# First sequence's q and k in 256-byte rows, and a written order for every early job, in a fused attention and feed-forward kernel

## The chip, the cores and the metric

The kernel runs on one core of one Trainium2 chip. The metric is device time in microseconds (us), from the first to the last instruction of the program with what lies around it. All data are 32-bit floats, except the two weight matrices, which arrive as 64-bit floats and are converted on the core.

## What is computed

Two blocks follow each other. The first is attention with a threshold: of each row of scores only those within `tau` of the row's maximum are kept.

```python
batch, n_heads, seq, head_dim = (8, 8, 576, 64)
scores = scale * np.matmul(q, k.transpose(0, 1, 3, 2))
thresh = np.max(scores, axis=-1, keepdims=True) - tau
scores = np.where(scores >= thresh, scores, -1000000000.0)
scores = scores - np.max(scores, axis=-1, keepdims=True)
attn = np.exp(scores)
attn = attn / (np.sum(attn, axis=-1, keepdims=True) + 1e-09)
out = np.matmul(attn, v)
```

The second is a feed-forward block over the 4608 tokens, with `w_in` of 512 x 2048 and `w_out` of 2048 x 512 (both float64):

```python
h = x @ w_in
g = np.where(h > 0.0, h, 1.0 * (np.exp(np.minimum(h, 0.0)) - 1.0))
return g @ w_out
```

## The kernel before

**Tiling.** Two heads make a pair, so there are 8 sequences x 4 pairs = 32 pairs. The 576 rows of a head are four blocks of 128 and a tail of 64, and the two tails of a pair share one step. A step is one block of 128 query rows of a pair: scores on TensorE (`sc`), maximum on VectorE (`max`), bound on GpSimd (`th`), exponential on ScalarE (`exp`), mask with the sum on VectorE (`mask`), sum and reciprocal, then the scaling of the row (`norm`). The weights so made are turned, either by TensorE (`part`, copied out of PSUM by `put`) or by VectorE in 32x32 squares with a trip through DRAM (`turn`, `send`, `landed`), and are multiplied with v (`val` early, `main` later). The results are copied out of PSUM by `values_out` (L733, L739).

**PSUM.** Three banks, `f0`, `f1`, `f2`, serve the feed-forward work. The other five are one tile, named `sc` (`wide[0]` in the code). In the front the scores of a step use its first four banks, and the fifth, called `t`, is lent out. From pair 4 on a tail step (`tails_and_values`, L708 scores, L713 and L721 values) uses banks 1 and 2 for the values of the pair two before it and banks 3 and 4 for its own scores. The scores of a half pair (`wide_scores`, L661) then use all five.

**Who waits for whom in the tile `sc`.** `on_banks` is the helper that all users of that tile pass through. It notes which of the five banks an instruction touches, adds a wait on the last users of those banks, and tells the framework to draw no others between these instructions. `watch` calls it where the destination may lie in that tile:

```python
def watch(made, ap):
    if ap.tensor.name == wide[0].tensor.name:
        on_banks(made, ap)
```

**The front.** The first sequence (pairs 0 to 3), the first two feed-forward chunks, the conversion of the 32 weight pieces and pairs 4 to 8 form the front. In it `early_tasks` keeps a table of jobs, each with an engine, a cost, a due time and what it needs. A list scheduler at build time picks, engine by engine, the next job, and `PR` holds its costs and due times. A weight piece i is `lw` (load, 512 KB), `shift`, `rest`, `add`, `sign`, `end` (L255, L244 or L249, L261, L266, L285). Where the plan of TensorE shows a gap, the scheduler fills it with transposes of the identity matrix that nobody reads (L465, `sc<-ident`, `f<-ident`). q and k are loaded as 32-element pieces of rows (128 bytes) by four DMAs to a tensor and pair (L303) and turned by VectorE (L329, L340). The feed-forward work of the front is 64 halves (L802, L774, L842). Twelve sums for a later stage (`xo`, L956) and 24 more (`in`, L928) run on GpSimd and VectorE.

**The loop.** From the tail step of pair 9 on a loop over the pairs takes over: tail step, `main` part 1, `main` part 0, `wide_scores` of half 0, 14 quarters of feed-forward products (L1491, L1631), `wide_scores` of half 1, 14 quarters. Everything that is not on TensorE is put on an agenda by its time after the matmuls (`at`), moved by the table `MOVED`, and issued in that order. The first matmuls of the values' two parts stand in this order, from `tail_step`:

```python
for part, cost in ((1, 2.2), (0, 1.8)):
    end = on_pe(cost, lambda: loc["main"](part))
    at(end, loc["outs"][part], f"out{part}")
```

In `MOVED` the copies out of part 1 stand at +0.83 us for odd pairs (`fout1`) and at -0.49 us for even ones (`sout1`); those of part 0 at -1.7 us for even ones (`sout0`).

Of the kernel before, what the change touches and what calls it, by code (L numbers as in the profile page):

```python
# [48 lines left out]
PR = {'wait_pe': 0.262,  # L49
 'wait_dve': 0.227,  # L50
 'wait_act': 0.276,
 'wait_pool': 0.0,
 'wait_sp': 0.0,
 'b0': 6.944,
 'p0': 4.249,
 'p1': 6.0,
 'p2': 24.241,
 'off': {'rest': -3.215,
         'prep': -4.66,
         'load': -4.611,  # L60
         'v': -4.074,
         'lw': -12.848,
         'crest': -2.529,
         'cadd': -2.278,
         'csign': -2.436,
         'cend': 9.54,
         'sc': -9.569,
         'max': -9.55,
         'exp': -2.54,
         'th': -3.219,  # L70
         'mask': -2.387,
         'norm': 1.617,
         'su': 3.77,
         'turn': 8.34,
         'fetch': 1.597,
         'part': 10.404,
         'put': 6.049,
         'val': 14.58,
         'valb': 7.639,
         'valsq': 3.622,  # L80
         'out': 2.393,
         'fexp': 7.269,
         'fmin': 1.493,
         'felu': 7.359,
         'fin': 1.533},
 'c0': 14.999,
 'c1': 3.798,
 'c2': 3.935,
 'in0': 13.65,
 'in1': 1.671,  # L90
 'xo0': 7.918,
 'xo1': 2.12,
 'h0': 62.091,
 'h1': 3.55,
 'ch0': 79.679,
 'ch1': 0.437,
 'rest_pool': [10, 11, 14, 22, 28, 3, 4, 6, 8],
 'in_pool': [[0, 0], [0, 1], [0, 2], [1, 1], [3, 1], [4, 0], [4, 1], [4, 2], [5, 0], [5, 1], [5, 2], [6, 0], [6, 1],
             [6, 2], [7, 0]],
 'act_norm': [[0, 0], [1, 0], [1, 1], [10, 0], [11, 0], [13, 0], [13, 1], [14, 0], [15, 1], [17, 0], [18, 0], [18, 1],  # L100
              [2, 0], [3, 0], [4, 0], [4, 1, 1], [4, 2, 0], [4, 4, 0], [5, 0, 0], [5, 1], [5, 1, 0], [5, 4, 0],
              [6, 0, 1], [6, 1, 1], [6, 2, 0], [6, 4, 0], [7, 2, 0], [7, 2, 1], [7, 3, 0], [7, 4, 0], [8, 1, 1],
              [8, 2, 0], [8, 2, 1], [8, 4, 0], [8, 4, 1]],
 'su_act': [[4, 0], [4, 1], [5, 2], [6, 0], [6, 1], [6, 2], [7, 0], [7, 4], [8, 2], 13, 14, 15, 2, 5, 7],
 'xo_n': 12,
 'jit': {},
 'split': 2,
 'warm': 83.985,
 'warm0': 8.0,
 'gap': 0.829,  # L110
 'keep': 0.583,
 'safe': 0.0,
 'idle': 20,
 'dma0': 1.287,
 'dma1': 306.761,
 'pt': 5.24,
 'ph': 9.482,
 'offb': {'prep': -6.011,
          'load': -12.705,
          'v': -14.084,  # L120
          'tail': -2.596,
          'wsc': 2.174,
          'main': 1.279,
          'outv': 3.527,
          'max': -0.056,
          'exp': -8.454,
          'th': 4.556,
          'mask': 4.757,
          'norm': 0.612,
          'su': 0.738,  # L130
          'turn': 4.815,
          'send': 1.309,
          'fetch': 20.101,
          'part': 13.644},
 'part_b': [[4, 0], [4, 2], [5, 1], [5, 2], [6, 3]],
 'squares': [12]}
# [3 lines left out]
def kernel(  # L140
# [19 lines left out]
    T = 32  # L160
# [25 lines left out]
    mains = {pr: wstage.tile([P, TAIL], FP32, name=f"qe{pr}", bufs=1) for pr in range(2)}  # L186
# [14 lines left out]
    pos, keep, far, ntau, ntau0 = (const.tile([P, 1], FP32, name=x) for x in ("pos", "keep", "far", "ntau", "ntau0"))  # L201

    def read_tau():
        nc.vector.tensor_scalar(pos, tau_sb, 0.0, None, ALU.is_ge)
        nc.vector.tensor_scalar(keep, pos, SCALE, None, ALU.mult)
        nc.vector.tensor_scalar(far, pos, -FAR, FAR, ALU.mult, ALU.add)
        nc.vector.tensor_tensor(ntau, tau_sb, far, ALU.max)
        nc.vector.tensor_scalar(ntau, ntau, -1.0, None, ALU.mult)
        nc.vector.tensor_scalar(ntau0, ntau, 1.0 / SCALE, None, ALU.mult)
# [10 lines left out]
    for t in qds + vds_first + vds:  # L220
        nc.gpsimd.memset(t, 0.0)
# [88 lines left out]
    def load_v(pr):  # L310
        b, j = divmod(pr, NPAIR)
        tiles = raws[pr]
        vm = tiles["vm"] = (wstage if pr < 2 else raw).tile([P, 2, NC, D], FP32, name="vm", bufs=2)
        vd = tiles["vd"] = (vds_first if pr < 2 else vds)[pr % NVD]
        for i in range(2):
            vh = v[b, 2 * j + i]
            nc.sync.dma_start(vm[:, i], vh[:MAIN].rearrange("(c p) d -> p c d", p=P))
            r = slice(i * TAIL, (i + 1) * TAIL)
            nc.sync.dma_start(vd[r, r], vh[MAIN:])

    def prep_q(pr):
        src = raws[pr]["qm"].rearrange("p j d -> p (j d)")
        if pr < 2:
            both = squares.tile([P, NT, NCH, T], FP32, name="x").rearrange("p g c n -> p (g c n)")
            qT, firsts[pr] = both[:, :MAIN], both[:, MAIN:]
        else:
            qT = qkp.tile([P, S], FP32, name="qT")
        n = (P, MAIN)[pr] if pr < 2 else S
        nc.vector.transpose(qT[:, :n], src[:, :n])  # L329
        if pr == 1:  # L330
            nc.vector.transpose(mains[pr], src[:, MAIN:])
        pairs[pr] = [qT, None, qds[pr % NQD]]

    def scale_q(pr):
        qT = pairs[pr][0]
        nc.gpsimd.tensor_scalar(qT, qT, keep, 1.0, ALU.mult, ALU.mult)

    def prep_k(pr):
        kT = pairs[pr][1] = firsts[pr] if pr < 2 else qkp.tile([P, TAIL + S], FP32, name="kT")
# [3 lines left out]
    def copy_q(pr):  # L343
        qT, _, qd = pairs[pr]
        for i in range(2):
            r = slice(i * D, (i + 1) * D)
            o, tail = qd[r, i * TAIL : (i + 1) * TAIL], mains[pr][r] if pr < 2 else qT[r, MAIN:]
            if pr == 1:
                nc.gpsimd.tensor_scalar(o, tail, keep[r], 1.0, ALU.mult, ALU.mult)
            else:  # L350
                nc.gpsimd.tensor_copy(o, tail)


    def copy_k(pr):
        kT = pairs[pr][1]
        nc.gpsimd.tensor_copy(kT[D:, :TAIL], kT[D:, S:])
# [18 lines left out]
    def vectors(pr):  # L375
        st = {x: small.tile([P, 2], FP32, name=x) for x in ("mx", "th", "su", "rs")}
        if not pr:
            st["nb"] = wstage.tile([P, 2], FP32, name="nb", bufs=4)
# [30 lines left out]
    def normalize_act(pr, i, h):  # L409
        st = open_steps[pr, i]  # L410
        wv = st["w"][:, h * S : (h + 1) * S]
        nc.scalar.mul(wv, wv, st["rs"][:, h : h + 1])
# [12 lines left out]
    def bound_of(pr, i, h):  # L425
        st = open_steps[pr, i]
        nc.gpsimd.tensor_scalar(st["th"][:, h : h + 1], st["mx"][:, h : h + 1], -1.0, ntau if pr else ntau0, ALU.mult,
                                ALU.add)

    def exp_of(pr, i, h):  # L430
        st = open_steps[pr, i]
        bias = st["mx"][:, h : h + 1]
        if not pr:
            bias = st["nb"][:, h : h + 1]
            nc.scalar.mul(bias, st["mx"][:, h : h + 1], keep)
        e = e_slot()
        o = st[h][:, :, :HALF]
        on_banks(nc.scalar.activation(e, o, AF.Exp, bias=bias, scale=1.0 if pr else keep), o)
# [25 lines left out]
    def transpose(dst, src):  # L464
        watch(nc.tensor.matmul(dst, src, idents[-1], is_transpose=True, skip_group_check=True), dst)  # L465
# [15 lines left out]
    def turn_parts(pr, i):  # L481
# [3 lines left out]
        def to(gs, cs, src, r=slice(0, P)):  # L485
            watch(nc.scalar.copy(wT[r, gs, cs].rearrange("p g c n -> p c g n"), src.rearrange("p c (g n) -> p c g n", n=T)), src)
# [4 lines left out]
        def chunks(c0, c1):  # L491
# [3 lines left out]
            return lambda: to(slice(g0, g0 + NT), slice(c0, c1), rt[:, : c1 - c0])  # L495
# [4 lines left out]
        def tails():  # L500
# [4 lines left out]
            def copies():  # L505
                to(ga, slice(0, NC), rt[:, :, :TAIL])
                to(gb, slice(NC + 1, NCH), rt[:, :, TAIL:])
# [3 lines left out]
        def common():  # L511
# [5 lines left out]
            def copies():  # L517
                cs = slice(NC, NC + 1)
                to(ga, cs, rt[:TAIL, :1, :TAIL], slice(0, TAIL))
                to(ga, cs, rt[TAIL:, 1:2, :TAIL], slice(TAIL, P))  # L520
                to(gb, cs, rt[:, 1:2, TAIL:])
# [6 lines left out]

    def turn(pr, i):
        for part in turn_parts(pr, i):  # L530
            part()()
# [65 lines left out]
    def values(pr, part, pv=None, block=None):  # L597
# [8 lines left out]
        watch(nc.tensor.matmul(pv[:, :n], vd, wT[:, :, NC], start=True, stop=False, skip_group_check=True), pv[:, :n])  # L606
        for c in range(NC):
            for h in range(2):
                g0, g1 = (2 * h, 2 * h + 10) if part else (0, wT.shape[1])
                o = pv[h * D : (h + 1) * D, g0 * T : g1 * T]  # L610
                watch(nc.tensor.matmul(o, vm[:, h, c], wT[:, g0:g1, h * (NC + 1) + c], start=False, stop=(c == NC - 1),
                                       skip_group_check=True), o)
        return lambda: values_out(pr, part, pv, block)
# [24 lines left out]
    def watch(made, ap):  # L638
        if ap.tensor.name == wide[0].tensor.name:
            on_banks(made, ap)  # L640

# [5 lines left out]
    def wide_scores(pr, half):  # L647

        qT, kT, _ = pairs[pr]
        for s in range(2):  # L650
# [5 lines left out]
        for h, s, c, n in ((0, 0, 0, 448), (1, 1, 0, 320), (1, 1, 320, 256), (0, 0, 448, 128),  # L656
                           (1, 0, 0, 256), (0, 1, 0, 384), (1, 0, 256, 320), (0, 1, 384, 192)):
# [27 lines left out]
    def tails_and_values(pr, before):  # L685
# [38 lines left out]
        return values_main, [lambda part=part: values_out(before, part, pv[:, part]) for part in range(2)]  # L724

    def values_out(pr, part, pv, block=None):
        b, j = divmod(pr, NPAIR)
        q0, n = TAIL * part, (3 if part else 2) * NT * T
        if block is not None:
            watch(nc.scalar.copy(xts[b][:, j, block * P : (block + 1) * P], pv[:, :P]), pv[:, :P])  # L730
            return
        o = pv[:, q0 : q0 + 2 * P]
        watch(nc.scalar.copy(xts[b][:, j, part * 2 * P : (part + 1) * 2 * P], o), o)  # L733
# [1154 lines left out]
```

## Time and profile before

| what | us |
|---|---|
| three timed runs | 1311.40, 1313.16, 1315.54 |
| median | 1313.16 |
| profiled execution, first to last instruction (its span) | 1310.6 |
| TensorE, VectorE, GpSimd, ScalarE busy | 1274.6, 1022.3, 782.7, 567.7 |
| first scores on TensorE | 5.96 |
| scores of step 4, of step 19 | 38.2, 126.3 |
| tail step of pair 9, where the loop starts | 288.62 |
| tail steps of pairs 10 and 11 | 327.27, 361.28 |

The profiled execution has no other time than its span; the median of the runs lies 2.56 us above it. All times below are counted from the span's first instruction. PE is TensorE, DVE VectorE, ACT ScalarE, POOL GpSimd, SP the engine that issues most DMAs; L and a number are a line of the kernel.

### The profile page before, as it was taken

What the parts mean: (1) busy time and instruction counts of PE and PEld (TensorE: products, weight loads), DVE (VectorE), ACT (ScalarE), POOL (GpSimd) and SP (SyncE); (2) the same over time, 40 slices, a digit from 0 to 9 for tenths busy, and PEclk for the clock granted to TensorE, in tenths of its full rate; (3) what the DMA queues carried; (4) which work ended last, traced back from release to release, by engine and by line L of the source; (5) the groups of instructions that cost most, each with busy time, mean ns of one, the idle gap of its engine ahead of it and who ended that gap; (6) DMA issues with size and microseconds to landing.
All of it is one profiled execution on the core that took longest, in us unless ns stands there. A gap on an engine that the chain in (4) does not pass through costs nothing.

```text
span 1310.6 us, 22008 instructions
## 1 busy us (share of the span) xinstructions
PE 1274.6 (97%) x6990; PEld 1002.2 (76%) x6990; DVE 1022.3 (78%) x2190; ACT 567.7 (43%) x1224; POOL 782.7 (60%) x1149
## 2 busy tenths in 40 slices
PE   7999989999999999999999999999999999999998
PEld 6677556447878888787878787878787887888887
DVE  5888768889889988898898979897989882545534
ACT  4778643445353444444443535252526260422320
POOL 3776583627657665767485747584758473624523
PEclk8999999999999999999999999999999999999999
DMA  7636678779898988898889898989889875221211
GB/s 142 168 119 177 169 208 239 219 213 264 228 254 221 258 230 237 222 244 244 245 215 253 243 235 228 261 240 246 234 239 258 220 218 179 93 73 58 96 61 33
DMA packets 334484, 261.66 MB, mean 200 GB/s; under 512 B 209952, under 2 KB 295456, under 8 KB 334368
## 3 DMA queue, kind: packets, MB, share of 16 engines
q1 hardware_dynamic: 332432, 259.78, 72.3%
q8 instruction: 55, 0.90, 0.3%
q10 hardware_dynamic: 1936, 0.48, 0.2%
q14 instruction: 61, 0.50, 0.1%
HBM read 168.76 MB, written 91.42 MB: 199 GB/s over the span
## 4 chain that ended last, share of the span: by engine, by line
PE 80%; DVE 7%; DMA 3%; POOL 3%; SPq 2%; ACT 2%; issue 2%; DVEq 0%; POOLq 0%; ACTq 0%
PE f L1631 29%; PE f L1491 28%; PE sc L721 8%; PE sc L661 8%; PE sc L713 2%; DVE mx L668 1%; DMA there<-x 1%; POOL t L956 1%; SPq L303 1%; PE sc L708 1%; PE sc L399 1%; PE f L802 1%; DMA wst<-in_moe_w_out_dram 1%; DVE w_one L682 1%; DVE x L539 1%
## 5 line engine op out<-in xcount | busy, mean ns | idle before, releaser
L668 DVE TENSOR_REDUCE mx<-sc 128x1 f32<-128x576 f32 x252 | 179.2, 748 | 32.5 <-PE sc L661 27.7
L678 ACT ACTIVATE w_one<-sc,mx 128x576 f32<-128x576 f32 x140 | 101.1, 739 | 137.5 <-DVE mx L668 114.0
L674 POOL TENSOR_SCALAR th<-mx,ntau 128x2 f32<-128x2 f32 (+1 forms) x140 | 41.6, 297 | 178.0 <-DVE mx L668 177.9
L407 POOL TENSOR_SCALAR w_one<-w_one,rs 128x576 f32<-128x576 f32 x137 | 111.9, 825 | 52.2 <-DVE rs L462 51.5
L661 PE MATMUL sc<-kT,qT 64*128 64x256 f32 (+5 forms) x896 | 127.0, 417 | 1.5 <-DVE w_one L682 1.5
L661 PEld LDWEIGHTS sc<-kT,qT 64*128 64x128 f32 x896 | 98.3, 186 | 35.2 <-issue 23.1
L1491 PE MATMUL f<-xt,sw 128*128 128x256 f32 x512 | 124.1, 384 | 0.8 <-ACT xt L733 0.5
L1491 PE MATMUL f<-xt,w_in_sb 128*128 128x256 f32 x512 | 122.2, 381 | 1.6 <-ACT g L1552 1.6
L682 DVE SCALAR_TENSOR_TENSOR w_one<-sc,th,w_one 128x576 f32<-128x576 f32 x140 | 109.7, 810 | 16.4 <-ACT w_one L678 12.1
L539 DVE STREAM_TRANSPOSE x<-w_one 128x512 f32<-128x512 f32 (+1 forms) x140 | 99.8, 743 | 20.7 <-POOL w_one L407 12.3
L1491 PEld LDWEIGHTS f<-xt,sw 128*128 128x128 f32 x512 | 93.7, 190 | 20.9 <-issue 5.0
L1491 PEld LDWEIGHTS f<-xt,w_in_sb 128*128 128x128 f32 x512 | 96.2, 190 | 17.1 <-ACT w L1505 2.5
L1631 PE MATMUL f<-w_out_sb,g 128*128 128x256 f32 x448 | 107.1, 382 | 0.0
L1631 PE MATMUL f<-w_out_sb,s 128*128 128x256 f32 x448 | 107.0, 382 | 0.0
L1631 PE MATMUL f<-t,s 128*128 128x256 f32 x448 | 105.8, 379 | 0.0
L1491 PE MATMUL f<-x,w_in_sb 128*128 128x256 f32 x448 | 105.8, 379 | 0.0
L678 ACT ACTIVATE e<-sc,mx 128x576 f32<-128x576 f32 x112 | 81.8, 743 | 53.2 <-DVE mx L668 51.6
L407 POOL TENSOR_SCALAR e<-e,rs 128x576 f32<-128x576 f32 x104 | 76.8, 742 | 40.4 <-DVE rs L462 39.1
L1578 POOL TENSOR_TENSOR s<-g 128x256 f32<-128x256 f32 x104 | 80.6, 781 | 28.1 <-PE f L1631 20.0
L682 DVE SCALAR_TENSOR_TENSOR e<-sc,th,e 128x576 f32<-128x576 f32 x112 | 87.9, 809 | 11.2 <-ACT e L678 8.8
L1631 PEld LDWEIGHTS f<-w_out_sb,g 128*128 128x128 f32 x448 | 84.1, 190 | 13.8 <-issue 2.9
L1631 PEld LDWEIGHTS f<-w_out_sb,s 128*128 128x128 f32 x448 | 84.2, 190 | 13.5 <-issue 2.5
(241 smaller groups left out, 2761.1 us busy)
## 6 DMA issues: line engine op xcount, KB each, us to landing
there<-x SPq DMA_DIRECT2D x444, 144.0 KB, 3.7
wTb<-there SPq DMA_DIRECT2D x56, 576.0 KB, 6.6
wTa<-there SPq DMA_DIRECT2D x55, 576.0 KB, 5.0
sw<-win_sums SPq DMA_DIRECT2D x62, 384.0 KB, 4.3
t<-wout_sums SPq DMA_DIRECT2D x45, 512.0 KB, 5.7
there<-x SPq DMA_DIRECT2D x112, 80.0 KB, 1.9
wTb<-there SPq DMA_DIRECT2D x56, 160.0 KB, 3.4
qm<-in_q_dram SPq DMA_DIRECT2D x124, 72.0 KB, 4.6
```

The costliest lines, as they stand in the source:

```text
L407: nc.gpsimd.tensor_scalar(wv, wv, st["rs"][:, h : h + 1], 1.0, ALU.mult, ALU.mult)
L539: nc.vector.transpose(x[:, :, c0 : c0 + nc_], src.rearrange("p (c g n) -> p g c n", c=nc_, n=T))
L661: on_banks(nc.tensor.matmul(o, qT[r, i * P : (i + 1) * P], kT[r, k0 : k0 + n], start=True, stop=True, skip_group_check=True), o)
L668: on_banks(nc.vector.tensor_reduce(st["mx"][:, h : h + 1], st["sc", h], axis=AX.XY if i == NC else AX.X, op=ALU.max, negate=True), st["sc" ...
L674: nc.gpsimd.tensor_scalar(st["th"][:, cs], st["mx"][:, cs], -1.0, ntau, ALU.mult, ALU.add)
L678: on_banks(nc.scalar.activation(st["e", h], st["sc", h], AF.Exp, bias=st["mx"][:, h : h + 1]), st["sc", h])
L682: on_banks(nc.vector.scalar_tensor_tensor(st["e", h], st["sc", h], st["th"][:, h : h + 1], st["e", h], ALU.is_ge, ALU.mult, accum_out=st[" ...
L713: on_banks(nc.tensor.matmul(o, vd[r, r], parts[x][r, g0:g1, NC], start=True, stop=False, skip_group_check=True), o)
L721: on_banks(nc.tensor.matmul(o, vm[:, h, c], parts[part][:, g0:g1, h * (NC + 1) + c], start=False, stop=(c == NC - 1), skip_group_check=Tru ...
L1491: nc.tensor.matmul(loc["banks"][place], left[:, j], right[:, j], start=(begins and j == 0), stop=(j == 1), skip_group_check=True)
L1578: engine.tensor_tensor(o, x, y, op)
L1631: nc.tensor.matmul(place(m), lhs, rhs, start=(begins and v == 0), stop=(v == RU - 1), skip_group_check=True)
```

## The change

The front is rewritten; the loop's own code is not, apart from helpers that it shares.

- All q and k of the first sequence are loaded in rows of 256 bytes into room that later holds `w_out`: k by two DMAs a pair, q by one DMA for each block of 128 rows of all heads, the tails by one DMA each. TensorE turns them (`turn_first`, `turn_first_tail`), and ScalarE or VectorE copies them out, q scaled at that moment. The first DMA is now the first weight piece.
- The scheduler, its costs and due times are gone. `EARLY` is a written list of 1276 entries that gives each early job its place and, after a colon, its engine; after an @ stands the PSUM bank. `follow` issues the jobs in that order. Entries such as `idle5@f2` are idle transposes: 14, 3, 8, 5, 5 and 4 of them at six places, all ahead of step 3's scores; there were 117.
- Copies out of PSUM can be done by ScalarE or VectorE (`copied`). 25 pieces' `rest` are on GpSimd where 9 were.
- `watch` is gone. Transposes, the values' matmuls of the front and all copies in `values_out` no longer pass through `on_banks`; the scores, the maximum, the exponential, the mask and the values' matmuls from pair 4 on still do.
- 28 jobs of the list have a bank `@t`; 29 with the idle transposes.

```diff
-PR = {'wait_pe': 0.262, 'wait_dve': 0.227, ...
+EARLY = """
+lw.0 ld.tau.0.0 idle14@f0 ld.k.0.0 ld.tail.1.0 ld.k.0.1 ld.q.0.0 shift.0 lw.1 ld.vd.3.0 sign.0 ld.k.1.1 rest.0
+first.t.k.3@f0 first.t.k.0@f1 ld.vd.2.1 copy.k.3:dve ld.k.1.0:act first.k.0.0@f2 tau ld.k.3.0 add.0 first.t.k.1@f0
+copy.k.0 ld.vd.0.0 prep.k.0.0 copy.k.1:dve ld.vd.2.0 first.q.0.0@f1 first.q.1.0@f0 prep.q.0.0:dve prep.q.1.0 ld.vd.1.1
+end.0 ld.k.2.0:act sc.0 shift.1 lw.2 first.q.2.0@f0 idle3@f2 max.0.0 ld.q.2.0 sign.1 ld.k.3.1 max.0.1 exp.0.0 th.0.0
+first.k.1.0@f1 ld.k.2.1 rest.1:pool first.t.k.2@f2 idle8@t exp.0.1 mask.0.0 th.0.1 add.1 prep.k.1.0 mask.0.1
...
+        def follow(order):
+            for entry in order.split():
+                x, _, e = entry.partition(":")
+                x, _, b = x.partition("@")
+                if b:
+                    granted[0] = places[b]
...
+    def turn_first(name, pr, chunks):
+        first_tiles(pr)
+        rt = granted[0]
+        for x, c in enumerate(chunks):
+            transpose(rt[:, x * P : (x + 1) * P], first_raw(name, pr, c))
...
+    def copied(engine, o, src):
+        return {"act": nc.scalar.copy, "dve": nc.vector.tensor_copy, "pool": nc.gpsimd.tensor_copy}[engine](o, src)
...
     def transpose(dst, src):
-        watch(nc.tensor.matmul(dst, src, idents[-1], is_transpose=True, skip_group_check=True), dst)
+        nc.tensor.matmul(dst, src, idents[-1], is_transpose=True, skip_group_check=True)
...
-    def watch(made, ap):
-        if ap.tensor.name == wide[0].tensor.name:
-            on_banks(made, ap)
...
-    def values_out(pr, part, pv, block=None):
+    def values_out(pr, part, pv, block=None, engine="act"):
...
         o = pv[:, q0 : q0 + 2 * P]
-        watch(nc.scalar.copy(xts[b][:, j, part * 2 * P : (part + 1) * 2 * P], o), o)
+        copied(engine, xts[b][:, j, part * 2 * P : (part + 1) * 2 * P], o)
         if part:
...
                 o = pv[r, h * (n - TAIL) : h * (n - TAIL) + TAIL]
-                watch(nc.scalar.copy(xs[r], o), o)
+                copied(engine, xs[r], o)
```

## The prediction

> **What bounds the kernel now.** I read the page's slices first, then the windows by stage, TensorE's waits, and the timeline around one tail step. Section 2 of the page:
>
> ```profile
> PE   7999989999999999999999999999999999999998
> DVE  5888768889889988898898979897989882545534
> PEclk8999999999999999999999999999999999999999
> ```
>
> TensorE is full after the first eighth of the span and little before it. The windows (us: busy time and instructions of PE, PEld, DVE, ACT, POOL; granted clock; DMA share; GB/s) cut at the first scores, step 4, step 19, and pair 9's tail step:
>
> ```profile
> 6.00:38.20 32.20, 26.48 (x189) 20.55 (x189) 20.26 (x48) 16.63 (x31) 12.46 (x24) 0.89 0.87 166
> 38.20:126.30 88.10, 80.41 (x591) 60.74 (x591) 75.77 (x157) 70.72 (x150) 65.41 (x85) 0.96 0.52 152
> 126.30:288.60 162.30, 149.10 (x688) 89.59 (x688) 130.72 (x278) 76.68 (x144) 88.50 (x127) 0.97 0.77 211
> 288.60:1080.00 791.40, 789.33 (x4444) 632.37 (x4446) 690.18 (x1520) 347.26 (x768) 519.35 (x775) 1.00 0.88 238
> ```
>
> Up to 38.2 us DMA is the fullest (0.87); between 38.2 and 126.3 VectorE is busy 86%; in the loop TensorE has 789 of 791 us. Asked who TensorE waited for between 330 and 1060 us, the waits answer with their heading alone:
>
> ```profile
> engine line waited for: us in total, times, longest us
> ```
>
> So two budgets count: the front ends at 288.62 us and can move, while in the loop each us that TensorE is made to wait is a us of the kernel. The timeline around pair 10's `main` (start, us, engine, line):
>
> ```profile
> 328.40 2.37 PE L721 MATMUL sc<-wTb,vm 128*64 128x320 f32 x16
> 330.61 1.90 PE L721 MATMUL sc<-wTa,vm 128*64 128x256 f32 x16
> 330.85 0.72 ACT L678 ACTIVATE w_one<-sc,mx 128x576 f32<-128x576 f32 x1
> 331.48 0.36 ACT L733 COPY xt<-sc 128x256 f32<-128x256 f32 x1
> 331.73 0.43 ACT L739 COPY xs<-sc 64x64 f32<-64x64 f32 x2
> 331.85 0.80 DVE L682 SCALAR_TENSOR_TENSOR w_one<-sc,th,w_one 128x576 f32<-128x576 f32 x1
> 332.43 2.21 PE L661 MATMUL sc<-kT,qT 64*128 64x448 f32 x16
> 332.55 0.37 ACT L733 COPY xt<-sc 128x256 f32<-128x256 f32 x1 [0.40 <-PE sc L721]
> ```
>
> The three copies of part 1 run beside part 0's matmuls, and part 0's copy runs beside the first scores. None delays TensorE. For pair 11, an odd one:
>
> ```profile
> 364.62 1.90 PE L721 MATMUL sc<-wTa,vm 128*64 128x256 f32 x16
> 364.84 0.37 ACT L733 COPY xt<-sc 128x256 f32<-128x256 f32 x1 [0.71 <-PE sc L721]
> 365.10 0.42 ACT L739 COPY xs<-sc 64x64 f32<-64x64 f32 x2
> 366.56 0.37 ACT L733 COPY xt<-sc 128x256 f32<-128x256 f32 x1 [1.03 <-PE sc L721]
> ```
>
> **The change, part by part: the loop.** The diff takes `watch` from the copies in `values_out`. Scores and masks still name their banks, but they exempt only instructions registered like them; the copies now count as users of the whole five-bank tile. The built programs' waits show it. Before, part 0's first matmul waits for no copy, and part 0's copy is first awaited by the half pair's fourth score matmul, as it works in bank 1. After, in even pairs part 0's first matmul waits for part 1's last copy; in odd pairs, whose copy is issued 0.83 us later (`fout1`), that copy waits for part 0's last matmul. In both the first score matmul waits for part 0's copy.
>
> Even pair: the last copy ends at 331.73 + 0.43 = 332.16; TensorE follows a releasing ACT copy by 0.06 (in the front L486 ends at 14.76, L606 starts at 14.82). Part 0 would start at 332.22, not 330.61: 1.61. It takes 332.43 - 330.61 = 1.82, its copy starts 0.12 after that (332.55), takes 0.37, and scores follow 0.06 later: 0.55. Sum 2.16. The mask, now also behind the copies, ends near 333.1, ahead of part 0.
>
> Odd pair: at part 0's end (366.45, where the scores start) all copies are still to do: 0.11 to the first, then steps of 0.26 and 0.42, 0.37 for the last, 0.06 back: 1.22.
>
> Loop pairs with scores behind are 9 to 31: 11 even x 2.16 + 12 odd x 1.22 = 38.4. Pair 32 pays the first wait only, about 1. Nothing hides this, as TensorE has no other wait there: **+39.4**. A wait of 1.6 could shrink if ScalarE were free sooner (its exponential at 330.85 is ahead of the copies); with the copies at once, as in pair 11, it would be 0.26 + 0.42 + 0.06 + 0.23 = 0.97, 0.64 less. So 32 to 40.
>
> The Trainium skill's page "PSUM — Partial Sum Buffer", section "PSUM bank collisions raise a hardware error", says to guard PSUM by bank, or bank and quadrant; a guard over five banks orders more than that needs. With a guard of that kind in the changed kernel the sum would be the front's alone, about 1311; its built program has the wider one.
>
> **The start.** Before, q and k come in 128-byte packets, 0.43 to 0.59 us an issue, four to a tensor. 32 such issues and more become 14, some 10 us less of SP's queue, on which the chain of waits lies for much of the first 38 us. But the first weight piece (landing 4.8 after issue, median) now goes first, near 0.73, and ScalarE's table load (1.28) waits for it. Then `sign` and `rest` (0.69 each), an issue (0.5), two copies (0.2 each) and the 512-column copy (0.59) stand ahead of step 0's scores: 0.73 + 4.8 + 1.28 + 1.38 + 0.5 + 0.4 + 0.59 = 9.7, against 5.96. Step 1: its k leaves ScalarE near 8.3, lands 3.2 later, and follows the masks: about 14.5 (before 17.0). SP stands behind the same landing, then issues five more: step 2 near 18 (26.9). Steps 3 and 4 at VectorE's pace, some 5.3 (two maxima 1.5, two masks 1.8, shift 0.56, end 0.83, small ones): step 4 near 28.6, not 38.2: **-9.6**.
>
> **Steps 4 to 19.** VectorE's sum hardly changes: 17 conversions end in this stage, 20 before (3 x 1.39 less), and a dozen copies of 0.2 to 0.6 come to it, about the same. The `rest` moved to GpSimd (16 x 0.70 = 11 over the front) are covered by its idle share there (65 of 88 us busy). The cost is bank t: its jobs count as users of the whole tile too. Step 4's first maximum waits for `val.1.block.0@t` behind the scores (0.42 + 1.02), step 5's second for a `part` (0.44); a copy of 0.59 is awaited likewise. 25 such jobs lie here. If VectorE's 12 us of idle time held them all: 0; at 1.4 each 35. I take **+10**: most wait 0.4 to 0.7, and half may coincide with conversions. Two conversions fewer are done at step 19: **+2.8** behind it.
>
> **From step 19 on.** In the chain 166 to 189 us lie mostly on GpSimd (twelve `xo` of about 1.3, `in` between). They are now spread up to pair 8: 0 to 10 gained; I take **-7**. Pairs 6 to 8 have the copies' waits, 3 x 1.2 = **+3.6** at most; half, as TensorE is idle 13 us there. The 39 idle transposes that remain (117 before) save nothing, being filler; 40 turning ones at 0.11 add 4.4 in idle time of the start.
>
> Sum of the front: -9.6 + 10 + 2.8 - 7 + 1.8 = -2, between -18 and +26. Span: 1310.6 - 2 + 39.4 = 1348; with the 2.56 between span and median **1350.6**.
>
> **Rivals.**
> - *The clock drops as well.* In the trace waits of 1.5 to 2.5 us in the front (at 60.4, 172, 200, 231) are each followed by 3.4 or 6.8 us at half clock, while 1.6 and 1.75 (124.6, 287) are not. If each even pair's wait did it, 11 x 1.7 = 19 more; all pairs, 39: 1369 to 1390. Against it: the waits are shorter than the sure ones. The Trainium skill's page "TensorE: Matmul & The Clock Gate", section "What's actually happening", has the clock drop after one idle window of about 3.4 us; by it no wait here costs clock, but this trace shows drops after shorter ones.
> - *The front pays for the loop; faster.* The place is VectorE in the front: 228 us of work in 288.6. If the written order filled it to 95% from about 7 us on, pair 9 would start at 247, 42 earlier, and the sum is 1311; it decides from a start before 249. Filled to 98%: 1304. For it: sums are spread and the start is early. Against: 28 jobs on bank t tie the engines to each other.
> - *Bank t costs its upper bound.* Then the front is 25 longer: 1376.
> - *The order does not do what it says.* "Idle transposes in all gaps" would remove the seven drops of the clock (about 1.7 each, 12 us): 1338. The list has none behind step 3, so those at 63, 176, 203 and 234 can remain.
>
> **How the numbers follow.** Forecast (loop 32 to 40, front -18 to +15) 0.64; clock 0.09; bank t 0.13; order fills gaps after all 0.06, inside the forecast's range; front pays for the loop 0.06, of which 0.05 end faster; 0.02 for the rest. Low end: 1313 + 32 - 18 = 1327. High: 1313 + 40 + 26 = 1379, which takes in bank t and leaves out most of the clock's case. 0.3% (4 us) is about what a measurement can tell: faster 0.05, same 0.03, slower 0.92.
>
> **What would show it.** TensorE's waits between pair 10 and pair 31 on `xt` and `xs` copies, L792 and L732, 1.2 to 1.6 and 0.5 each; a period of the tail steps of 35.7 instead of 34.05. The front: first scores near 9.7, step 4 near 29, pair 9 near 287. I am wrong if the period stays 34.05, or if pair 9 starts before 250.

## The result, and the profile after

| | runs, us | median | ratio to before |
|---|---|---|---|
| before, on the same chip | 1311.40 to 1315.54 (4) | 1314.09 | |
| changed kernel | 1371.53 to 1373.28 (4) | 1372.78 | 1.0446, 95% interval 1.0431 to 1.0461 |

The changed kernel is slower by 58.7 us; 37.4 were forecast. The profiled execution's span is 1371.5 us.

The slices of the page, for the three rows shown of before:

```profile
PE   7778899999999999999999999999999999999998
DVE  5666798888878887888788878897888873445534
PEclk9899999999999999999999999999999999999999
```

Each slice is 34 us now. VectorE's second to fifth slices showed 8, 8, 8, 7 before; here they show 6, 6, 6, 7. The front has become thinner, not fuller.

The windows, cut at step 4's first maximum (37.7 us, before 40.7), the tail step of pair 4 (163.5, before 144.0), and that of pair 9 (308.7, before 288.6); columns: busy time and instructions of PE, PEld, DVE, ACT, POOL, granted clock, DMA share, GB/s:

```profile
6.00:37.70 31.70, 23.75 (x153) 16.60 (x154) 20.77 (x55) 18.01 (x33) 12.19 (x19) 1.00 0.89 207
37.70:163.50 125.80, 97.36 (x658) 72.65 (x658) 84.82 (x180) 70.19 (x148) 63.71 (x87) 0.91 0.35 98
163.50:308.70 145.20, 137.35 (x627) 84.63 (x627) 124.42 (x268) 73.11 (x134) 87.10 (x120) 0.96 0.83 227
308.70:1100.00 791.30, 755.61 (x4225) 601.54 (x4224) 654.42 (x1448) 325.64 (x717) 491.74 (x738) 1.00 0.85 229
```

The second and third of these stages in the kernel before:

```profile
40.70:144.00 103.30, 94.29 (x684) 70.78 (x681) 86.07 (x175) 81.69 (x173) 74.30 (x95) 0.97 0.55 156
144.00:288.60 144.60, 132.72 (x587) 78.10 (x586) 118.07 (x254) 64.23 (x118) 78.34 (x117) 0.96 0.77 215
```

Two rows carry the loss. In the second, no engine is full: VectorE works 84.8 of 125.8 us, where it worked 86.1 of 103.3. In the last, a window of the loop as long as the one shown of before, TensorE has 755.6 us where it had 789.3, so 34 us more of idle time. What it waited for between pair 10 and pair 31 (before, this list was empty):

```profile
engine line waited for: us in total, times, longest us
PE sc L732 <- ACT xt L421: 17.1, 21, 1.2
PE sc L792 <- ACT xs L421: 15.9, 11, 1.5
```

These are the two waits of the forecast, and there is no third. Between the tail steps of pairs 10 and 31 the changed kernel takes 37.65 us more: 33.2 us are idle time of TensorE, and 4.5 us a longer busy time for the same matmuls (719.6 against 715.1). That is 0.14 us for each of the 32 waits; what lengthens them was not tried. The timeline around pair 10's `main`, an even pair:

```profile
351.58 0.36 ACT L421 COPY xt<-sc 128x256 f32<-128x256 f32 x1
351.83 0.43 ACT L421 COPY xs<-sc 64x64 f32<-64x64 f32 x2
...
352.31 1.95 PE L792 MATMUL sc<-wTa,vm 128*64 128x256 f32 x16 [1.45 <-ACT xs L421]
...
354.31 0.37 ACT L421 COPY xt<-sc 128x256 f32<-128x256 f32 x1 [2.05 <-PE sc L792]
...
354.73 1.03 PE L732 MATMUL sc<-kT,qT 64*128 64x448 f32 x5 [0.47 <-ACT xt L421]
```

Part 0's matmuls (bank 1) start 0.05 us after part 1's last copy (bank 2), and the scores 0.05 us after part 0's copy. Before, part 0's ran beside the one and the scores beside the other. Pair 11, an odd one, has all three copies between its matmuls and its scores:

```profile
388.86 0.37 ACT L421 COPY xt<-sc 128x256 f32<-128x256 f32 x1 [2.43 <-PE sc L792]
389.13 0.42 ACT L421 COPY xs<-sc 64x64 f32<-64x64 f32 x2
389.58 0.37 ACT L421 COPY xt<-sc 128x256 f32<-128x256 f32 x1
390.00 2.21 PE L732 MATMUL sc<-kT,qT 64*128 64x448 f32 x16 [1.19 <-ACT xt L421]
```

In the front, VectorE's waits between step 4 and the tail step of pair 4 (the first five rows of the list):

```profile
DVE mx L506 <- PE sc L685: 12.2, 5, 3.9
DVE mx L506 <- PE sc L543: 8.3, 8, 2.8
DVE w L526 <- ACT e L516: 4.1, 4, 2.6
DVE w_one L526 <- PE sc L543: 3.1, 3, 1.5
DVE mx L506 <- ACT wTb L421: 2.7, 5, 1.2
```

L685 and L543 with `sc` are values and transposes in bank `t`, L421 their copies: maxima (L506) and masks (L526) of scores in other banks wait for them. The longest of these waits in the timeline:

```profile
97.08 1.24 PE L482 MATMUL sc<-x,qf 128*128 128x288 f32 x4 [0.63 <-ACT wTb L421]
...
98.16 0.81 PE L680 MATMUL sc<-wTb,vf 128*128 128x384 f32 x2
...
98.90 2.38 PE L685 MATMUL sc<-wTb,vm 128*64 128x320 f32 x16
101.38 0.74 ACT L516 ACTIVATE e<-sc,mx 128x576 f32<-128x576 f32 x1 [3.61 <-PE sc L685]
101.39 0.76 DVE L506 TENSOR_REDUCE mx<-sc 128x1 f32<-128x576 f32 x1 [3.95 <-PE sc L685]
```

The scores first wait 0.63 us for a copy out of `t`. They are done at 98.3, their maximum starts at 101.39: 18 value matmuls in `t` lie between, and both this maximum and the exponential of the step before stand behind them.

### The profile page after: what moved, and what is told of

It reads as the page before. It is cut to its first block, busy times and chain, and to the rows that moved or that the text cites. A ratio compares the mean times of both kernels' runs of the same rounds, so it can differ in the third digit from the quotient of the medians.

```text
span 1371.5 us, 21875 instructions
## 1 busy us (share of the span) xinstructions
PE 1280.4 (93%) x6952; PEld 1002.6 (73%) x6952; DVE 1019.5 (74%) x2206; ACT 563.7 (41%) x1212; POOL 776.1 (57%) x1141
## 4 chain that ended last, share of the span: by engine, by line
PE 62%; DVE 13%; POOL 7%; ACT 6%; DMA 5%; issue 4%; SPq 1%; DVEq 0%; ACTq 0%; POOLq 0%
PE f L1512 28%; PE f L1372 12%; PE sc L732 7%; PE sc L792 6%; DMA wTb<-there 3%; DVE mx L739 3%; POOL w_one L490 2%; DVE e L753 2%; PE sc L482 2%; ACT xt L421 1%; PE f L851 1%; PE f L919 1%; POOL u L1391 1%; DVE g L1422 1%; PE sc L685 1%
## 5 line engine op out<-in xcount | busy, mean ns | idle before, releaser
L732 PE MATMUL sc<-kT,qT 64*128 64x320 f32 (+5 forms) x896 | 129.4, 429 | 26.4 <-ACT xt L421 26.0
L732 PEld LDWEIGHTS sc<-kT,qT 64*128 64x128 f32 x896 | 102.6, 193 | 60.3 <-ACT xt L421 37.8
L490 POOL TENSOR_SCALAR w_one<-w_one,rs 128x576 f32<-128x576 f32 x115 | 89.2, 786 | 40.6 <-DVE rs L540 40.6
L1512 PE MATMUL f<-t,s 128*128 128x256 f32 x448 | 105.8, 379 | 0.0
L1372 PE MATMUL f<-x,w_in_sb 128*128 128x256 f32 x448 | 105.8, 379 | 0.0
L1459 POOL TENSOR_TENSOR s<-g 128x256 f32<-128x256 f32 x104 | 80.8, 783 | 27.9 <-PE f L1512 20.1
L1372 PEld LDWEIGHTS f<-x,w_in_sb 128*128 128x128 f32 x448 | 85.1, 190 | 11.6
## 6 DMA issues: line engine op xcount, KB each, us to landing
there<-x SPq DMA_DIRECT2D x444, 144.0 KB, 3.8
```

What stands on the lines that cost most here:

```text
L490: nc.gpsimd.tensor_scalar(wv, wv, st["rs"][:, h : h + 1], 1.0, ALU.mult, ALU.mult)
L732: on_banks(nc.tensor.matmul(o, qT[r, i * P : (i + 1) * P], kT[r, k0 : k0 + n], start=True, stop=True, skip_group_check=True), o)
L1372: nc.tensor.matmul(loc["banks"][place], left[:, j], right[:, j], start=(begins and j == 0), stop=(j == 1), skip_group_check=True)
L1459: engine.tensor_tensor(o, x, y, op)
L1512: nc.tensor.matmul(place(m), lhs, rhs, start=(begins and v == 0), stop=(v == RU - 1), skip_group_check=True)
```

## Experiments

All kernels were run beside the kernel before, whose median was 1313.2 to 1315.0 each time. "Named" means that an instruction passes through `on_banks` again. An instruction so named is exempt from every order against the group, also from the true ones on other tiles; where transposes or copies of the front are named, two such orders are therefore written by hand: a mask behind the last transpose that read its tile, and values behind the copies that filled theirs.

The period is the mean time from one tail step to the next between pairs 10 and 31. Two theories stood against each other. *Whole-tile orders*: the loss is the lost naming, in loop and front. *The written order*: the loop's loss is the naming, the front's belongs to the new list of jobs.

**1. Everything named**

```diff
+    def watch(made, ap, also=()):
+        if ap.tensor.name == wide[0].tensor.name:
+            on_banks(made, ap, also)
-        nc.tensor.matmul(dst, src, idents[-1], is_transpose=True, skip_group_check=True)
+        made = nc.tensor.matmul(dst, src, idents[-1], is_transpose=True, skip_group_check=True)
+        watch(made, dst)
...
-        copied(engine, xts[b][:, j, part * 2 * P : (part + 1) * 2 * P], o)
+        watch(copied(engine, xts[b][:, j, part * 2 * P : (part + 1) * 2 * P], o), o)
```

> The changed kernel with the bank naming put back on every transpose, value matmul and copy that works in the five-bank tile (and the two true waits that the naming would hide written by hand: a mask behind the last transpose that read its tile, values behind the copies that filled theirs). Theory 'orders on the whole tile': both losses go, the loop's (37.65 us between pair 10 and pair 31, about 40 with pairs 9 and 32) and the front's; pair 9's tail step near 284, time 1305 to 1316. Rival 'the written order itself': the loop's 40 us go, but the front keeps its 20; pair 9's tail step at 309, time near 1333. Rival 'something else in the loop': period of the tail steps stays near 35.8 and the time above 1345.

Measured: 1290.3 us, ratio to before 0.9815 (0.9795 to 0.9835). Both losses are gone, and more: pair 9's tail step is at 264.3, some 20 us earlier than even the first theory gave. The windows, cut at the same events as above, and VectorE's waits in the second of them (the longest rows):

```profile
6.00:31.40 25.40, 21.69 (x138) 15.48 (x138) 21.41 (x55) 17.79 (x33) 12.10 (x19) 0.87 1.06 246
31.40:123.50 92.10, 86.05 (x673) 66.38 (x672) 85.16 (x181) 67.87 (x144) 65.11 (x88) 1.00 0.50 137
123.50:264.30 140.80, 135.46 (x629) 80.56 (x627) 124.44 (x268) 73.67 (x137) 86.90 (x120) 1.00 0.85 231
264.30:1020.30 756.00, 753.23 (x4229) 603.12 (x4228) 658.52 (x1448) 325.20 (x717) 495.12 (x738) 1.00 0.89 240
```

```profile
DVE w_out_sb L310 <- POOL wtop L286: 1.5, 1, 1.5
DVE w L527 <- ACT e L517: 1.4, 3, 0.9
```

The same VectorE work (85.2 us, 84.8 in the changed kernel) takes 92.1 us instead of 125.8: idle time 6.9 instead of 41.0. So the new front without the lost names is faster than the old one by 24.4 us. That is the order together with all else that changed in the front (256-byte loads, TensorE turning q and k, jobs on other engines); these were not tried apart.

**2. Only the loop's copies named** (`values_out`, pairs from 4 on)

> The changed kernel with the bank naming put back only on the copies of values_out from pair 4 on (loop copies). Orders on the whole tile: period of the tail steps back to 34.05, no wait of TensorE on xt and xs copies between pair 10 and 31, pair 9's tail step still at 309: 1372.8 - 40 = 1333. If the loop's loss came from elsewhere: 1365 or more.

Measured: 1332.8 us. The period of the tail steps is 34.11 us (changed kernel 35.85, before 34.05), and TensorE's waits on copies between pairs 10 and 31 are gone:

```profile
engine line waited for: us in total, times, longest us
PE f L1380 <- DMA sw<-win_sums: 0.9, 2, 0.6
```

The loop's part is 1372.8 - 1332.8 = 40.0 us.

**3. Only the first sequence's work named**

> The changed kernel with the naming put back only on the first sequence's work in the five-bank tile (transposes, their copies, value matmuls, their copies). Orders on the whole tile: the front loses the waits of VectorE on bank t jobs (24 us of them between 40 and 126 us), pair 9's tail step near 284 to 290, loop period 35.8 as in the changed kernel: 1347 to 1354. Rival 'the written order itself': pair 9 at 309 as now, 1372.

Measured: 1332.6 us, pair 9 at 269.9, period 35.80. The front's names are worth 40.2 us, about twice what was expected: the loss was expected to be what the front is behind the old one, and it hides a gain.

**4. Before, with the loop's copies unnamed**

```diff
-        watch(nc.scalar.copy(xts[b][:, j, part * 2 * P : (part + 1) * 2 * P], o), o)
+        made = nc.scalar.copy(xts[b][:, j, part * 2 * P : (part + 1) * 2 * P], o)
+        if pr < NPAIR:
+            watch(made, o)
```

> The kernel before with only the naming of the loop copies (values_out, pairs from 4 on) taken away, front and order as they were. Orders on the whole tile: the loop pays 2.2 us in an even and 1.2 us in an odd pair; period 35.8, pair 9 within 3 us of 288.6: 1314 + 38 to 42 = 1352 to 1356. If part of the changed kernel's loop loss came from its other order, less than 1345.

Measured: 1355.2 us, 40.4 more than before; period 35.80. TensorE's waits between 360 and 1015 us:

```profile
PE sc L661 <- ACT xt L733: 14.9, 18, 1.2
PE sc L721 <- ACT xs L741: 12.8, 9, 1.4
```

In the same stretch of the changed kernel they are 15.0 (18 times) and 13.0 (9). The loop's loss is this edit and nothing else. Pair 9 came at 292.9, 4.3 later than before; 3.5 of that stand already at pair 4's tail step, ahead of every edited copy, so one execution's front can differ from another's by that much.

**5. Before, with nothing of this named**: `watch` does nothing.

> The kernel before, its loads and its order as they were, with no copy, transpose or early value matmul naming its banks (the naming edit of the change alone). Whole-tile orders, independent of the order of jobs: the loop pays the 40 us it paid when only its copies lost their names, and the front pays besides; its built program has 57 more false waits that involve the early jobs, the changed kernel 71 with 40 us paid, so about 32: 1315 + 40 + 32 = 1387 (1370 to 1400). Rival 'the front's loss belongs to the written order and its jobs in the fifth bank': the old front stays within 5 us, 1355 to 1360.

Measured: 1381.8 us, 67.2 more than before; pair 9 at 318.4. The old front loses too, 26.8 us beside the loop's 40.4. The four corners, in us:

| | named | not named | the names are worth |
|---|---|---|---|
| old front | 1314.5 | 1381.8 | 67 |
| new front | 1290.3 | 1372.8 | 82 |

**6. More idle transposes, loop's copies named**: `idle10` in a free bank ahead of 12 of the scores of steps 4 to 19.

> The changed kernel with the loop's copies named (1332.8) and ten idle transposes more ahead of 12 of the 16 scores jobs of steps 4 to 19, each in a bank that is free there, so that TensorE does not stand still before them. If the clock drops of the front (granted 0.55 between 40 and 50 us, 0.72 and 0.79 between 90 and 110 in the changed kernel, some 24 us at half clock) carry part of the front's 40 us: 5 to 9 us less, about 1326. If the waits alone carry them: 1333, or up to 8 more where the transposes themselves stand in the way.

Measured: 1339.3 us, 6.4 more than without them. It does not answer the question on the clock: between 40 and 126 us the granted clock is 0.88, against 0.85 without, as the transposes themselves waited for their banks (1.7 and 1.4 us in all on copies to `wTb` and `wTa`). It shows that filler in TensorE's queue is not free where its bank is awaited.

**7. Everything named, no idle transposes**: the six `idle` entries are struck out.

> The changed kernel with all banks named (1290.3), without its 39 idle transposes. If they hold the clock up in the start: granted clock lower in the first 50 us and 2 to 8 us slower, 1292 to 1298. If they are filler only: 1290.

Measured: 1293.7 us (1289.9 to 1294.7), against 1290.3 (1290.0 to 1291.4): not told apart by the times, whose intervals (0.9806 to 0.9870 and 0.9795 to 0.9835) overlap. The traces differ as expected: granted clock 0.89 between 20 and 50 us instead of 1.00, VectorE busy 25.75 instead of 28.85 us there, step 4's first maximum at 34.7 instead of 31.4, pair 9 2.3 us later.

**8. Everything named, first weight piece later**

```diff
-lw.0 ld.tau.0.0 idle14@f0 ld.k.0.0 ld.tail.1.0 ld.k.0.1 ld.q.0.0 shift.0 lw.1 ...
+ld.tau.0.0 idle14@f0 ld.k.0.0 ld.tail.1.0 ld.k.0.1 ld.q.0.0 lw.0 lw.1 ...
```

> The changed kernel with all banks named, and the first weight piece loaded behind the first sequence's first k, q and tails instead of ahead of them, its three conversion steps behind the copies of step 0. If the piece's landing sets the first scores (10.2 us), these come near 6.5 us and the front starts up to 3.7 us earlier, of which VectorE, then full, keeps 1 to 3.7: 1287 to 1289. If VectorE's sum alone counts (the first conversion is only moved back): 1290 or a little more.

Measured: 1291.7 us, no gain. The first scores start at 8.97 instead of 10.55 us, not at 6.5: k lands only 1.1 us earlier. The first maximum comes later (13.53 instead of 12.84), as `end.0`, which waits for GpSimd until 12.59, stands ahead of it in VectorE's order.

**9 and 10. Loop's copies named, and one half of the front**: the values with their copies (9), or the transposes with theirs (10).

> The changed kernel with the loop's copies (1332.8) and the first sequence's value matmuls and their copies named; the transposes into the fifth bank and their copies are not. If the long jobs carry the front's 42 us (eight values jobs of 1.4 to 3.2 us, each awaited by the next maximum): 1300 to 1310. If it goes by the number of jobs (20 transposing jobs against 8 values): 1320. The two splits should add up to about 42.

> The changed kernel with the loop's copies (1332.8) and the transposes into the fifth bank and their copies named; the value matmuls of the first sequence and their copies are not. If the long jobs carry the front's 42 us: 1320 to 1325. If it goes by the number of jobs: 1303.

Measured: 1306.7 and 1304.9 us. (There are 9 values jobs and 19 transposing ones in `t`, not 8 and 20.) From step 4 to the tail step of pair 4, the windows of run 2, run 9 and run 10:

```profile
40.90:166.40 125.50, 98.17 (x656) 72.59 (x656) 84.79 (x180) 70.17 (x148) 63.57 (x87) 0.90 0.33 94
```
```profile
34.40:139.10 104.70, 90.48 (x675) 68.70 (x674) 84.52 (x181) 68.84 (x144) 65.06 (x88) 0.97 0.43 120
```
```profile
34.40:140.30 105.90, 89.00 (x656) 66.69 (x656) 85.15 (x180) 69.08 (x147) 64.14 (x87) 0.98 0.43 117
```

VectorE's work is the same in all; its idle time is 40.7, 20.2 and 20.8 us, and 6.9 with everything named. By the times, the transposes alone cost 1306.7 - 1290.3 = 16.4 us (0.9 a job), the values alone 14.6 (1.6 a job), and both together 42.5: 11.5 more than their sum. The two splits do not add up to 42 as expected, so neither of the two ideas of a price per job holds. The clock differs too: by the granted clock over these stages (0.90, 0.97, 0.98, and 1.00 in run 1) some 25, 6, 4 and 0 us were at half clock.

**11 and 12. Everything named, the start once more**: as 8, with `end.0` behind step 0's two maxima (11), and with 28 idle transposes at the start for 14 (12).

> As the kernel with the later first weight piece, and the end of that piece's conversion now also behind step 0's two maxima in VectorE's order, ahead of which it stood waiting for GpSimd (12.59 us). If the start is worth something to a full VectorE: first maximum near 11.5 instead of 12.8 to 13.5, pair 9's tail step 1 to 2 us earlier than 264.3, time 1287 to 1289. If VectorE's sum alone counts: 1290 to 1291.

> The same with 28 instead of 14 idle transposes at the start, so that TensorE does not stand still between 4.7 and 6.1 us. If that gap drops the clock for step 0 (eight score matmuls in 2.29 us, 0.47 us a transpose): these at full clock, first maximum 1.2 to 2 us earlier still, time 0 to 2 us less than without. If not: the same time.

Measured: 1289.7 us (1288.6 to 1293.7) and 1287.4 (1286.9 to 1288.1), ratios to before 0.9830 (0.9817 to 0.9844) and 0.9805 (0.9791 to 0.9818). In 11 the first maximum is 1.3 us earlier than in run 1, step 4's 0.3, pair 9 0.6: the start is worth next to nothing, as it would be if VectorE's sum decides. Run 12 is the fastest of all, but hardly by its start: its step 0 scores take 1.24 us instead of 2.29, yet begin at 10.08 instead of 9.23, as the idle transposes hold TensorE until 7.54 while in run 11 the first turning of k starts at 6.39. So the first maximum is only 0.2 us earlier (11.3). The two kernels stand at 208.2 and 208.0 us at pair 7, then at 236.5 and 233.2 at pair 8. It is run 11 that stands out: it takes 28.3 us between these two tail steps, runs 1, 7 to 10 and 12 take 25.2 to 26.2. In run 11 TensorE waits 2.3 us in pair 7's tail step, and the granted clock is half from 212.1 to 215.5 us; in run 12 its only wait there is 0.8 us and the clock stays full. So part of the 2.3 us between the two medians may come from there and not from the start; why the wait differs was not tried.

## Why the prediction was right, and where it was not

The sign, the main mechanism and the range held; the time came out 22 us above the forecast, nearly all of it in the front. Both parts ended above the bands of the forecast that was given 0.64 (loop 40.8 against 32 to 40, front +20.1 against -18 to +15): the time lies in the range because its upper end took in bank `t`. Pair 9's tail step was put 2 us earlier than before and came 20 later (308.7 against 288.6). The steps, with run 1 to part what the new front does from what the lost names do; the front is cut at pair 4's tail step, not at step 19:

| step of the sum | forecast | measured | from |
|---|---|---|---|
| loop behind pair 9 | +39.4 | +40.8 | span less pair 9: 1062.8, before 1022.0 |
| start, up to step 4 | -9.6 | -9.3 | first maximum of step 4: 31.4 in run 1, before 40.7 |
| step 4 to pair 4, the new front itself | 0 | -11.2 | step 4 to pair 4's tail step: 92.1 in run 1, before 103.3 |
| bank `t` | +10, bound 35 | +40.0 | pair 4's tail step: 163.5, in run 1 123.5; 6.3 of it stand at step 4 already |
| behind that, new front (-7 and +2.8) | -4.2 | -3.8 | pair 4 to pair 9: 140.8 in run 1, before 144.6 |
| copies of pairs 6 to 8 | +1.8 | +4.4 | the same stretch: 145.2 |

- **The loop.** Right by its steps: 1.45 us on average for the even pairs' first wait, 1.2 at most for the scores, period 35.85 against 35.7. Pair 9 pays nothing (38.7 us to pair 10, before 38.7), where 1.22 was put. From pair 31 to the end it is 3.1 us longer (271.3 against 268.2), where 2.2 was put for pairs 31 and 32.
- **Bank `t` is the step that failed.** It was priced at 10 us, from 0.4 to 0.7 us a job, and halved because "half may coincide with conversions". Its bound of 35, 25 jobs at 1.4, was too low as well. (21 of the 25 stand between the scores of steps 4 and 19, the other four up to pair 4's tail step.) The front's bounds, -18 and +26, are not what its own terms give: these are -16.8 with the best of each, and +31.8 with bank `t` at 35, nothing gained behind step 19 and the copies in full. Two things were missing. First, hardly anything coincides when the order is written: a conversion that stands behind a waiting maximum in VectorE's list cannot step forward, so the waits become idle time of the fullest engine (41.0 us idle, where run 1 has 6.9). Second, the price was that of one link, scores to maximum. A job in `t` is a link both ways: it waits for the exponential, maximum or mask before it, TensorE keeps its order, the next scores stand behind it, and the next maximum behind both. Runs 9 and 10 show a surplus: 16.4 and 14.6 alone, 42.5 together. The timeline at 97 to 101 us shows such links, but that they make the surplus is argued, not shown. The clock has a part in the 40 us, and perhaps in the surplus, that was not isolated: granted 0.91 over this stage is some 23 us at half clock (125.8 x 0.09 x 2), which would cost up to half of that.
- **The start** was right in size, -9.3 with everything named. In the changed kernel itself step 4's maximum is only 2.9 us earlier (37.7), and its scores start at 33.5, where 29 was forecast (run 1: 29.6); bank `t` is in use from step 0 on (`idle8@t`). Its working was right by luck in one place: the first scores came at 10.2, near the 9.7 of the forecast, but run 8, where the weight piece comes later, starts them only 1.6 us earlier: most of the way from 5.96 to 9.7 was not the piece.
- **Steps 4 to 19 without the names** were put at VectorE's old pace, as its sum hardly changes. In the new front it is 92% busy (85.2 of 92.1 us) instead of 83% (86.1 of 103.3), worth 11 us.
- **Rival: the clock drops as well.** It did not happen: the granted clock is 1.00 over the loop, with 32 waits of up to 1.5 us in it. By the rule of the Trainium skill's page "TensorE: Matmul & The Clock Gate", section "What's actually happening", waits as short as these do not cost the clock; the trace agrees for the loop. The clock record changes only in steps of 3.41 us. In each such step of the loop TensorE works 2.2 us or more, while right before the four drops of the kernel before between 60 and 240 us it works 1.9, 1.4, 0.9 and 1.2 us. No limit follows from this, as one drop in the changed kernel's front (105.8) comes behind a step with 2.2 as well.
- **Rival: the front pays for the loop.** Its mechanism, a front that fills VectorE better, is real and was hidden under bank `t`. In run 1 VectorE is busy 92% from step 4 to pair 4, yet pair 9 starts at 264, not 247, since from pair 4 to pair 9 VectorE is 88% busy (124.4 of 140.8).
- **Rival: bank `t` at its upper bound**, 1376 at 0.13, was the nearest to what happened (1372.8).
- **Rival: the order does not do what it says.** "Idle transposes in all gaps" are not there, and with the names they aren't missed: granted clock 1.00 from 31 to 264 us in run 1.
- The rule of the Trainium skill's page "PSUM — Partial Sum Buffer", section "PSUM bank collisions raise a hardware error", to guard PSUM by bank, was said to leave the front's sum alone, about 1311. Run 1 is that kernel, at 1290.3: with the names, bank `t` and the copies of pairs 6 to 8 cost nothing (10 + 1.8 had been left in the sum), and the new front brings 11 more.

## What to carry to other kernels

A wait between two engines on data that they do not share is a chain, not a delay: price it by the idle time that it can leave on the fullest engine of its stage, at full length and with what is queued behind it on both sides, and do not halve it for chance cover when the order of every queue is fixed. When a change has a good part and a bad one, build the two single parts before you judge either: here the new front is worth 24 us, and the lost bank names cost 82. A helper that looks like bookkeeping, such as a list of banks that an instruction touches, can be worth more than the schedule around it.

## What the runs showed of the hardware

The granted clock that the profile shows for the first microseconds is not always what the matmuls run at. Step 0's eight score matmuls in runs 11, 1 and 12, in this order:

```profile
9.23 2.29 PE L483 MATMUL sc<-x 64*128 64x288 f32 x8
```
```profile
10.55 2.29 PE L483 MATMUL sc<-x 64*128 64x288 f32 x8
```
```profile
10.08 1.24 PE L483 MATMUL sc<-x 64*128 64x288 f32 x8
```

The granted clock at these places reads 1.00 in run 11, 0.50 in run 1 and 1.00 in run 12; by the durations it was half in the first two. In run 11 the trace has no clock record ahead of 14.11 us, and the windows read 1.00 all the same. (In the changed kernel the first record is at 13.62 us, so the 1.00 of its first window is no better.) Where the record is missing, the duration of a known matmul tells more.

The first 14 idle transposes take 3.25 us (1.46 to 4.71), after which TensorE stands still until k lands. In run 1 this did bring the clock up, but only for one step of the record, from 4.65 to 8.06 us: the first four 128x128 transposes of k take 0.75 us, and the scores behind them are slow again. In run 11 the clock did not come up: the same four take 1.11 us. With 28, TensorE is busy from 1.46 to 7.54, the record reads 1.00 from 7.25 on, and step 0 runs at full speed. Counted back from the first record in steps of 3.41 us, the 14 transposes fill 3.19 us of one step in run 1 (1.24 to 4.65) and 2.41 us at most in run 11 (0.45 to 3.87). The Trainium skill's page "TensorE: Matmul & The Clock Gate", section "What's actually happening", has a cold TensorE come to full clock only after some 3.4 us of sustained work, by a window that runs freely; these three runs agree with it.
